# Pooled attention and a maxout FFN on one core: another fold of the first keys, chosen slots for the attention steps, one batch of loads at a time and five store buffers

## The chip, the cores and the metric

The kernel runs on 1 core of one Trainium2 chip. The metric is the device time of one execution in microseconds; less is better. The chip has eight cores, and seven stay idle here. A core has five engines that run beside one another, each with its own queue of instructions in a fixed order: TensorE (PE, matmuls; PEld are its weight loads), VectorE (DVE), ScalarE (ACT), GpSimd (POOL) and SyncE (SP), which here only issues transfers. Engines wait for one another by semaphores.

## The reference

```python
def _attn_ref(q, k, v):              # each 8 x 8 x 576 x 64: batch, heads, tokens, width
    pool = 8
    k_p = k.reshape(B, H, Sp, pool, D).mean(axis=3)      # Sp = 72
    v_p = v.reshape(B, H, Sp, pool, D).mean(axis=3)
    scores = scale * np.matmul(q, k_p.transpose(0, 1, 3, 2))
    scores = scores - np.max(scores, axis=-1, keepdims=True)
    attn = np.exp(scores)
    attn = attn / (np.sum(attn, axis=-1, keepdims=True) + 1e-09)
    return np.matmul(attn, v_p)

def _moe_ref(x, w1, w2, w3, w_out):  # x is 4608 x 512, w1..w3 512 x 768, w_out 768 x 512
    h = np.maximum(np.maximum(x @ w1, x @ w2), x @ w3)
    return h @ w_out
```

`x` is the output of the attention, its heads side by side: 8 batches of 576 tokens make 4608 rows. Keys and values are averaged over groups of 8 tokens, so a head has 72 of each. Inputs and output are float32.

## The kernel before

**Tiles.** The FFN runs over nine tiles of 512 tokens (`n` = 0 to 8), the attention over eight batches of 576 tokens. The loop for tile `n` also does the attention of batch `n + 1`, so that TensorE has dense work in between. Tiles 7 and 8 have no attention beside them.

**Attention of a batch.** `fold_k` and `fold_v` add the eight tokens of a group in three halvings; batch 0's keys on VectorE in three thirds (line 327), batches 2 to 7 on GpSimd, while `pool_k` and `pool_v` sum k and v of batch 1 and v of batch 0 by eight accumulating matmuls with an identity. `kp` holds the pooled keys twice; `turn_k` transposes them on TensorE into `pkt` and copies that into `kz` on two sets of rows, one after the other. `turn_q` transposes blocks of 128 queries into `pqt` and copies them to `qT`. `scores` makes one head's scores in `psc` and ScalarE's exponential writes them to `et`. `values` multiplies `et` with the pooled values (a column of eights gives the sum), and VectorE takes the reciprocal `rcp` and writes the scaled `xn`. `turn_x` transposes `xn` into `pxt` and ScalarE copies it to `xT`, the FFN's input.

**FFN of a tile.** `hidden` has a slot for each of 6 blocks of 128 hidden units and each of the three weight matrices: four accumulating matmuls into `pw`, then a copy on ScalarE (first matrix) or a maximum on VectorE (second and third, the third into `hT`). That is 18 slots; for tiles 0 and 1 the first two blocks run in two halves of 256 tokens, so that there are 24. `project` has four slots: six matmuls into `po`, a copy on ScalarE into the store buffer `osb` and two stores of 128 KB from SP (line 311).

**Banks and buffers.** PSUM has eight banks: three for `pw`, `po` and the start's transposes, two buffers of two banks ("att") for `psc` and `pav`, and one ("tr") that `pqt`, `pkt`, `pxt` and the poolings of batch 1 share. `osb` lies in a pool with three buffers (`sb3`, line 306); `kt`, `vt` and `qb` have two each.

**The order** is written by hand: the program order is the order in each engine's queue. Attention steps are generators that yield after each step; `queries(b)` followed by `outputs(b)` are 22 steps for a batch. Lines 401 to 424 take one step after each of the 22 slots of a tile (`todo`), in tile 1 only after six slots (`lead`), and after every slot a step of what is left over from batch 1 (`side`). At the start, `heat` runs matmuls on constant data into a bank that nobody reads.

**Loads.** q, k, v and weights are loaded from GpSimd's queue, which also folds; k 0, k 2 and v 2 come from SP. Ahead of the loop the loads of batches 3 and 4 are issued, and in the loop those of batch `n + 4` (lines 402 to 411), each behind the fold that frees its buffer.

Of the kernel before, what the change touches and what calls it, by code (L numbers as in the profile page):

```python
# [10 lines left out]
ALU = mybir.AluOpType  # L11
# [3 lines left out]
def kernel(  # L15
# [30 lines left out]
    JCH = DFF // 128  # L46
# [27 lines left out]
    def load_v(b, eng, dtype=F32, parts=1):  # L74
        vts[b] = ld.tile([Sp, H, POOL, D], dtype, name="vt", tag="vt")
        src = v[b].rearrange("h (sp j) d -> sp h j d", j=POOL)
        n = H // parts
        return [eng.dma_start(out=vts[b][:, h:h + n], in_=src[:, h:h + n])
                for h in range(0, H, n)][-1]
# [22 lines left out]
    nc.vector.memset(warm, 1.0)  # L102
    ident = const.tile([128, 128], BF16, name="ident", tag="ident")
    make_identity(nc, ident)
    load_v(0, nc.gpsimd, F16, 2)
    identh = const.tile([128, 128], F16, name="identh", tag="identh")
    make_identity(nc, identh)
    for i in range(3):
        load_w(slice(256 * i, 256 * i + 256))
    load_k(1, nc.gpsimd, F16)  # L110
# [31 lines left out]
    def fold_v(b):  # L142
        fold(nc.gpsimd, vts[b], [vp_all[:, b, :, 0:D]])

    def pool_v(b, h, tag, evac):

        pvp = psp.tile([128, 4, D], F32, name="pvp", tag=tag[0], bufs=tag[1])
        for j in range(POOL):
            nc.tensor.matmul(pvp, identh[0:Sp, :], vts[b][:, h:h + 4, j, :],  # L149
                             start=(j == 0), stop=(j == POOL - 1))  # L150
        evac(out=vp_all[:, b, h:h + 4, 0:D], in_=pvp[0:Sp])

    def turn_q(b, n0, n1, evac, tag):
        if b not in qTs:
            qTs[b] = sb2.tile([128, 2 * NG, 128], BF16, name="qT", tag="qT")
        pqt = psp.tile([128, n1 - n0, 128], BF16, name="pqt", tag=tag[0],
                       bufs=tag[1])
        qf = qbs[b].rearrange("p hp t d -> p (hp t d)")
        for n in range(n0, n1):
            nc.tensor.transpose(pqt[:, n - n0, :], qf[:, 128 * n:128 * n + 128],  # L160
                                ident)
        evac(out=qTs[b][:, n0:n1, :], in_=pqt)  # L162

    def turn_k(b, evacs, tag):
        pkt = psp.tile([128, 6, 96], BF16, name="pkt", tag=tag[0], bufs=tag[1])
        for i in range(6):
            nc.tensor.transpose(pkt[:, i, :], kps[b][:, i, :, :], ident[0:96, 0:96])  # L167
        for par in range(2):
            rows = slice(64 * par, 64 * par + 64)
            evacs[par](  # L170
                out=kz_all[b % 2][rows, par, :, 0:Sp].rearrange(
                    "p h (r i) -> p h r i", i=6),
                in_=pkt[rows].rearrange("p i (h r) -> p h r i", h=H))
# [58 lines left out]
    TR = ("tr", 1)  # L232
# [3 lines left out]
    def queries(b):  # L236

        new_et(b)
        if b == 1:
            pool_k(b, TR)  # L240
            yield
            turn_k(b, V_V, TR)
            yield
        for m in range(3):
            turn_q(b, 6 * m, 6 * m + 6, nc.scalar.copy, TR)
            yield
        if b > 1:
            turn_k(b, V_V, TR)
            yield
        for h in range(H):  # L250
            scores(b, h)
            yield
# [45 lines left out]
    def project(n, hT):  # L298
        for mm in range(4):
            m = 4 * n + mm  # L300
            po = psp.tile([128, C], F32, name="po", tag="pw", bufs=3)
            for jc in range(JCH):
                nc.tensor.matmul(po, hT[:, jc, bass.ts(mm, 128)],  # L303
                                 wo_sb[:, jc, :],
                                 start=(jc == 0), stop=(jc == JCH - 1))
            osb = sb3.tile([128, C], F32, name="osb", tag="osb")
            nc.scalar.copy(out=osb, in_=po)  # L307
# [12 lines left out]
    def heat(n):  # L320
        for _ in range(n):
            nc.tensor.matmul(wm, warm[:, 0:128], warm, start=True, stop=True)

    new_et(0)
    heat(14)
    for i in (0, 2, 4):
        fold_k(0, nc.vector, i, i + 2)
    turn_q(0, 0, 5, nc.scalar.copy, PW)
    turn_q(0, 5, 9, nc.scalar.copy, PW)
    heat(1)  # L330
    turn_k(0, (nc.vector.tensor_copy, nc.scalar.copy), PW)

    def scores4(h):
        psc = psp.tile([128, 4, 256], F32, name="psc4", tag="att", bufs=2)
        for i in range(4):
            score(0, h + i, psc[:, i, :], 0, 0, 4)
        exp(ets[0][:, h:h + 4, 0:256], psc[0:Sp])

    def scores2(h):
# [12 lines left out]
    pool_v(0, 0, PW, nc.vector.tensor_copy)  # L352
    scores2(2)
    pool_v(0, 4, PW, nc.vector.tensor_copy)
    scores2(4)
    heat(1)
    scores2(6)
    out0 = outputs(0, (PW, PW, TR, TR, TR))
    next(out0)
# [8 lines left out]

    nc.vector.memset(kz_all[1], 0.0)
    hT0 = new_hT()  # L370
    side = queries(1)
    steps = {16: 1, 17: 1, 19: 1, 20: 1, 21: 1, 22: 2, 23: 2}
# [5 lines left out]
    pool_v(1, 0, TR, nc.scalar.copy)  # L378
    next(side)
    next(side)  # L380
    pool_v(1, 4, TR, nc.scalar.copy)
    for _ in side:
        pass
    side = outputs(1)
# [16 lines left out]
    NSTEP = 3 + 1 + H + 5 + 5  # L401
    for n in range(1, TOK // NB):
        if n + 2 < B:
            fold_k(n + 2, nc.gpsimd)
            if n + 4 < B:
                load_k(n + 4, nc.gpsimd)
            fold_v(n + 2)
            if n + 4 < B:
                load_v(n + 4, nc.gpsimd)
        if n + 3 < B:  # L410
            load_q(n + 3)
        hT = new_hT()
        nxt = batch(n + 1) if n + 1 < B else iter(())
        lead = 6 if n == 1 else 0
        nslot = 3 * JCH + 4
        slot = -lead
        for part in (hidden(n, hT), project(n, hT)):
            for _ in part:
                next(side, None)
                if slot >= 0:  # L420
                    todo = (slot + 1) * NSTEP // nslot - slot * NSTEP // nslot
                    for _ in range(todo):
                        next(nxt, None)
                slot += 1
        for _ in nxt:
            pass
# [30 lines left out]
```

## Time and profile before

| what | us |
|---|---|
| median of 3 runs | 284.22 |
| the three runs | 282.95, 284.22, 291.58 |
| the profiled execution | 282.14 |
| its span | 280.3 |

| engine | busy us | share of the span | instructions |
|---|---|---|---|
| PE | 254.8 | 91% | 1837 |
| PEld | 139.3 | 50% | 1838 |
| DVE | 129.9 | 46% | 232 |
| ACT | 132.2 | 47% | 224 |
| POOL | 117.7 | 42% | 83 |

The span is what the hardware profiler saw between the first and the last instruction; the time of an execution has 1.8 us around it. The trace has starts and lengths of instructions, and for an engine that sat idle, what released it. The page cuts the span into 40 slices of 7 us: TensorE's and the DMA engines' busy share in tenths, and the clock that TensorE was granted. The DMA engines are busy in the first half and TensorE has holes in three places, the first two slices, slices 13 and 14, and the last one:

```profile
PE   7689999788992699999999999999999999999993
PEclk9799999999999599999999999999999999999998
DMA  7999998898999989979006500600060006006006
```

### The profile page before, as it was taken

The numbers are of one execution on the slowest core, as the hardware profiler recorded it, in microseconds if no ns is written. First come the engines' busy times: TensorE is split into PE (matmuls) and PEld (weight loads), VectorE is DVE, ScalarE is ACT, GpSimd is POOL, SyncE is SP. The second block draws the span as 40 slices with busy tenths as digits, with TensorE's granted clock in tenths as the row PEclk, the third lists the DMA queues.
The fourth block names the chain that finished last, engine by engine and source line by source line (L and its number), as shares of the span: only waits on it lengthen the run. The fifth ranks groups of instructions, "written<-read, shape, count | busy, mean of one in ns | idle before, by whom it ended". The sixth has DMA issues, their size and how long they took to land.

```text
span 280.3 us, 4602 instructions
## 1 busy us (share of the span) xinstructions
PE 254.8 (91%) x1837; PEld 139.3 (50%) x1838; DVE 129.9 (46%) x232; ACT 132.2 (47%) x224; POOL 117.7 (42%) x83
## 2 busy tenths in 40 slices
PE   7689999788992699999999999999999999999993
PEld 2468457564551345554555455545554554444441
DVE  5547553434640055625562556255625562531530
ACT  1464257555540456465646554655456544124122
POOL 8551004999699999938940993000000000000000
PEclk9799999999999599999999999999999999999998
DMA  7999998898999989979006500600060006006006
GB/s 184 201 196 206 201 237 190 217 235 146 207 227 238 263 183 188 225 183 210 14 4 150 84 4 2 150 0 0 10 143 2 0 13 139 0 1 152 0 1 150
DMA packets 20850, 34.71 MB, mean 124 GB/s; under 512 B 2620, under 2 KB 13244, under 8 KB 20252
## 3 DMA queue, kind: packets, MB, share of 16 engines
q0 software_dynamic: 14032, 21.44, 40.5%
q1 hardware_dynamic: 6796, 12.98, 19.2%
q8 instruction: 14, 0.23, 0.3%
q14 instruction: 8, 0.07, 0.1%
HBM read 34.60 MB, written 9.44 MB: 157 GB/s over the span
## 4 chain that ended last, share of the span: by engine, by line
PE 79%; DMA 9%; ACT 5%; DVE 4%; issue 2%; SPq 0%; ACTq 0%; POOLq 0%
PE pw L273 46%; PE po L303 14%; DMA out_dram<-osb 6%; PE psc L189 6%; DVE kz L170 3%; PE pqt L160 3%; PE pav L218 3%; PE pxt L209 3%; DMA qb<-in_q_dram 3%; ACT qT L162 2%; PE pvp L149 1%; PE pkt L167 1%; ACT t L278 1%; ACT xT L213 1%; ACT osb L307 1%
## 5 line engine op out<-in xcount | busy, mean ns | idle before, releaser
L273 PE MATMUL pw<-xT,mw 128*128 128x512 f16 (+1 forms) x696 | 161.5, 366 | 0.9 <-ACT xT L213 0.7
L273 PEld LDWEIGHTS <-mw 128*128 128x128 f16 x696 | 61.4, 98 | 47.7 <-issue 2.2
L281 DVE TENSOR_TENSOR t<-t,pw 128x512 f16<-128x512 f16 (+1 forms) x58 | 37.8, 651 | 80.6 <-PE pw L273 43.6
L303 PE MATMUL po<-mwo,hT 128*128 128x512 f16 x216 | 51.7, 379 | 0.1
L194 ACT ACTIVATE et<-psc 72x576 f16<-72x576 f32 (+2 forms) x62 | 40.4, 662 | 23.2 <-PE psc L189 23.0
L278 ACT CAST t<-pw 128x512 f16<-128x512 f32 (+1 forms) x58 | 32.3, 557 | 36.1 <-PE pw L273 33.0
L284 DVE TENSOR_TENSOR hT<-t,pw 128x512 f16<-128x512 f16 (+1 forms) x58 | 37.7, 650 | 18.5 <-PE pw L273 16.9
L128 POOL TENSOR_TENSOR vt<-vt 72x2048 f32<-72x2048 f32 (+1 forms) x12 | 41.2, 3433 | 2.8 <-DMA vt<-in_v_dram 2.3
L307 ACT COPY osb<-po 128x512 f32<-128x512 f32 x36 | 21.1, 586 | 44.2 <-PE po L303 31.7
L128 POOL TENSOR_TENSOR kt<-kt 96x1536 f32<-96x1536 f32 (+1 forms) x12 | 31.5, 2621 | 23.5 <-DMA kt<-in_k_dram 22.9
L213 ACT COPY xT<-pxt 128x512 f16<-128x512 f16 (+1 forms) x40 | 21.8, 546 | 19.4 <-PE pxt L209 19.4
L189 PE MATMUL psc<-qT,kz 128*128 128x64 bf16 (+3 forms) x192 | 27.1, 248 | 3.8 <-DVE kz L170 3.6
L303 PEld LDWEIGHTS <-hT 128*128 128x128 f16 x216 | 19.4, 97 | 19.3 <-DVE hT L284 0.7
L226 DVE TENSOR_TENSOR xn<-pav,rcp 128x512 f16<-128x512 f32 x40 | 27.7, 692 | 1.4
L189 PEld LDWEIGHTS <-kz 128*128 128x128 bf16 x192 | 17.6, 98 | 21.2 <-DVE kz L170 7.8
L162 ACT COPY qT<-pqt 128x768 bf16<-128x768 bf16 (+2 forms) x23 | 18.0, 786 | 17.4 <-PE pqt L160 17.4
L160 PE MATMUL pqt<-ident,qb 128*128 128x128 bf16 x144 | 13.3, 235 | 11.9 <-ACT xT L213 8.2
L160 PEld LDWEIGHTS <-qb 128*128 128x128 bf16 x144 | 10.9, 105 | 19.7 <-issue 14.8
L218 PEld LDWEIGHTS <-et 72*128 72x128 f16 x320 | 15.4, 98 | 8.3 <-issue 0.7
L224 DVE RECIPROCAL rcp<-pav 128x8 f32<-128x8 f32 x40 | 8.1, 204 | 24.3 <-PE pav L218 24.3
L209 PEld LDWEIGHTS <-xn 128*128 128x128 f16 x160 | 12.1, 98 | 10.6 <-issue 1.9
L218 PE MATMUL pav<-vp,et 72*128 72x65 f16 x320 | 16.8, 194 | 0.3 <-ACT et L194 0.3
(38 smaller groups left out, 111.4 us busy)
## 6 DMA issues: line engine op xcount, KB each, us to landing
out_dram<-osb SPq DMA_DIRECT2D x72, 128.0 KB, 2.4
kt<-in_k_dram POOLq DMA_DIRECT2D x5, 1152.0 KB, 11.9
vt<-in_v_dram POOLq DMA_DIRECT2D x5, 1152.0 KB, 12.7
qb<-in_q_dram POOLq DMA_DIRECT2D x7, 576.0 KB, 13.0
mw<-in_moe_w_dram POOLq DMA_DIRECT2D x9, 256.0 KB, 10.5
kt<-in_k_dram SPq DMA_DIRECT2D x3, 384.0 KB, 5.2
kt<-in_k_dram SPq DMA_DIRECT2D x1, 1152.0 KB, 10.4
vt<-in_v_dram SPq DMA_DIRECT2D x1, 1152.0 KB
```

What stands on the lines that cost most here:

```text
L128: e.tensor_tensor(out=t[:, :, 0:n, :], in0=t[:, :, 0:n, :], in1=t[:, :, n:2 * n, :], op=ALU.add)
L160: nc.tensor.transpose(pqt[:, n - n0, :], qf[:, 128 * n:128 * n + 128], ident)
L189: nc.tensor.matmul(out, kz_all[b % 2][:, f % 2, h, :], qTs[b][:, n + i0:n + i1, 64 * (h % 2):64 * (h % 2) + 64], start=True, stop=True)
L194: nc.scalar.activation(out=out, in_=in_, func=FT.Exp, scale=1.0 / 64.0)
L213: nc.scalar.copy(out=xT[:, :, g0 + keep:g0 + 128], in_=pxt[:, :, keep:128])
L218: nc.tensor.matmul(pav[:, h // 4, 65 * (h % 4):65 * (h % 4) + 65], ets[b][:, h, c0:c0 + 128], vp_all[:, b, h, :], start=True, stop=True)
L226: nc.vector.tensor_tensor(out=xn, in0=pv[:, :, :, 0:D], in1=rcp.to_broadcast([128, 2, 4, D]), op=ALU.mult)
L273: nc.tensor.matmul(pw, w_sb[wi][:, kc, bass.ts(jc, 128)], xT[:, kc, col], start=(kc == 0), stop=(kc == KCH - 1))
L278: nc.scalar.copy(out=t, in_=pw)
L281: nc.vector.tensor_tensor(out=t1, in0=t, in1=pw, op=ALU.max)
L284: nc.vector.tensor_tensor(out=hT[:, jc, c0:c1], in0=t, in1=pw, op=ALU.max)
L303: nc.tensor.matmul(po, hT[:, jc, bass.ts(mm, 128)], wo_sb[:, jc, :], start=(jc == 0), stop=(jc == JCH - 1))
```

## The change

It has four parts.

1. **Store buffers.** The tile `osb` is given five buffers instead of three.
2. **Loads.** The loads of batch 4 ahead of the loop are gone. In the loop, `fold_k(n + 2)` is followed by the load of k for batch `n + 3`, `fold_v(n + 2)` by those of v and q for batch `n + 3`.
3. **Slots.** A batch's queries are turned in four groups (5, 5, 4, 4 blocks) instead of three of 6, with the keys between the third and the fourth, so a batch has 23 steps. The lists `PLAN` and `PLAN1` (tile 1) name the slot of each step; the two steps that are left of batch 1 come after slots 0 and 2 of tile 1. For batch 1, in tile 0, the keys still come first, in slots 16 and 17, the four query groups in 19 to 22, two scores in 23 and six behind the last slot (before: three groups, two scores in slot 22, two in 23, four behind).
4. **Start.** k of batch 0 is folded once on VectorE (three adds of 4 tokens onto 4, into `k16`, float16), and the four sums are added by four matmuls with an identity per third. `spread` copies them to the two places of `kp` on VectorE and ScalarE. The keys are turned before the queries, the second half of q after the first four scores; v of batch 0 comes in three transfers and is pooled in three pieces. `heat` matmuls stand in between.

```diff
+    def load_v(b, eng, dtype=F32, cuts=(0, H)):
...
-    load_v(0, nc.gpsimd, F16, 2)
     identh = const.tile([128, 128], F16, name="identh", tag="identh")
     make_identity(nc, identh)
+    load_v(0, nc.gpsimd, F16, (0, 4, 6, 8))
...
     def queries(b):
         new_et(b)
-        if b == 1:
-            pool_k(b, TR)
-            yield
-            turn_k(b, V_V, TR)
-            yield
-        for m in range(3):
-            turn_q(b, 6 * m, 6 * m + 6, nc.scalar.copy, TR)
+        for m, (n0, n1) in enumerate(((0, 5), (5, 10), (10, 14), (14, 18))):
+            turn_q(b, n0, n1, nc.scalar.copy, TR)
             yield
-        if b > 1:
-            turn_k(b, V_V, TR)
-            yield
+            if m == 2 and b > 1:
+                turn_k(b, V_V, TR)
+                yield
...
-            osb = sb3.tile([128, C], F32, name="osb", tag="osb")
+            osb = sb3.tile([128, C], F32, name="osb", tag="osb", bufs=5)
...
+    def spread(i0, i1):
+        nc.vector.tensor_copy(out=kps[0][:, i0:i1, 0, :], in_=pkp0[0:96, i0:i1])
+        nc.scalar.copy(out=kps[0][:, i0:i1, 1, :], in_=pkp0[0:96, i0:i1])
+
     for i in (0, 2, 4):
-        fold_k(0, nc.vector, i, i + 2)
+        c = slice(i, i + 2)
+        nc.vector.tensor_tensor(out=k16[:, c], in0=kts[0][:, c, 0:4],
+                                in1=kts[0][:, c, 4:8], op=ALU.add)
+        for j in range(4):
+            nc.tensor.matmul(pkp0[:, c], identh[0:96, :], k16[:, c, j, :],
+                             start=(j == 0), stop=(j == 3))
+        if i == 2:
+            spread(0, 4)
+        else:
+            heat(1)
+    spread(4, 6)
+    heat(2)
+    turn_k(0, (nc.vector.tensor_copy, nc.scalar.copy), PW)
     turn_q(0, 0, 5, nc.scalar.copy, PW)
-    turn_q(0, 5, 9, nc.scalar.copy, PW)
-    heat(1)
-    turn_k(0, (nc.vector.tensor_copy, nc.scalar.copy), PW)
+    turn_q(0, 5, 9, nc.vector.tensor_copy, PW)
...
+    scores4(0)
     turn_q(0, 9, 14, nc.vector.tensor_copy, PW)
-    scores4(0)
     turn_q(0, 14, 18, nc.vector.tensor_copy, PW)
...
-    load_k(4, nc.gpsimd)
-    load_v(4, nc.gpsimd)
...
+    PLAN = (1, 2, 4, 5, 7, 8, 9, 10, 11, 12, 13, 14, 15, 16, 17, 17, 18, 18, 19, 19,
+            20, 20, 21)
+    PLAN1 = (7, 8, 10, 13, 14, 15, 16, 17, 18, 19, 20, 21, 22, 23, 24, 24, 25, 25, 26,
+             26, 27, 27, 27)
     for n in range(1, TOK // NB):
         if n + 2 < B:
             fold_k(n + 2, nc.gpsimd)
-            if n + 4 < B:
-                load_k(n + 4, nc.gpsimd)
+            if n + 3 < B:
+                load_k(n + 3, nc.gpsimd)
             fold_v(n + 2)
-            if n + 4 < B:
-                load_v(n + 4, nc.gpsimd)
-        if n + 3 < B:
-            load_q(n + 3)
+            if n + 3 < B:
+                load_v(n + 3, nc.gpsimd)
+                load_q(n + 3)
```

The rows below are instructions in the order of one engine's queue: source line, operation, output and inputs, shape; x2 stands for two alike in a row. The lines of the changed kernel differ from those of before by a few.

ScalarE at the start, from its first copy to the first three exponentials, before:

```order
L162 COPY qT<-pqt 128x640
L162 COPY qT<-pqt 128x512
L170 COPY kz_120<-pkt 64x8x72
L194 ACTIVATE et<-psc_186 72x4x256
L194 ACTIVATE et<-psc_199 72x4x256
L194 ACTIVATE et<-psc_205 72x2x320
```

and in the changed kernel:

```order
L326 CAST kp<-pkp 96x4x64
L326 CAST kp<-pkp 96x2x64
L169 COPY kz_121<-pkt 64x8x72
L161 COPY qT<-pqt 128x640
L193 ACTIVATE et<-psc_192 72x4x256
L193 ACTIVATE et<-psc_212 72x4x256
```

Two casts of `kp` came in front, the query copy moved behind the `kz` copy, and the second query copy went to VectorE.

ScalarE at the end of tile 0, from the last FFN copies to the first store buffers, before:

```order
L162 COPY qT<-pqt 128x768 x2
L278 CAST t_536<-pw_531 128x512
L162 COPY qT<-pqt 128x768
L194 ACTIVATE et<-psc 72x576 x4
L151 CAST vp<-pvp 72x4x64
L194 ACTIVATE et<-psc 72x576 x2
L151 CAST vp<-pvp 72x4x64
L194 ACTIVATE et<-psc 72x576 x2
L307 COPY osb<-po 128x512 x2
```

and in the changed kernel:

```order
L161 COPY qT<-pqt 128x640 x2
L272 CAST t_556<-pw_551 128x512
L161 COPY qT<-pqt 128x512 x2
L193 ACTIVATE et<-psc 72x576 x3
L150 CAST vp<-pvp 72x4x64
L193 ACTIVATE et<-psc 72x576 x2
L150 CAST vp<-pvp 72x4x64
L193 ACTIVATE et<-psc 72x576 x3
L301 COPY osb<-po 128x512 x2
```

There are four query copies instead of three, and one exponential less ahead of the first `vp` cast and one more behind the second.

VectorE at the end of tile 2, from the maximum of a late FFN slot through the values of batch 3, before:

```order
L284 TENSOR_TENSOR hT<-t_1317,pw_1324 128x512
L224 RECIPROCAL rcp<-pav 128x8
L226 TENSOR_TENSOR xn<-pav,rcp 128x512
L281 TENSOR_TENSOR t_1360<-t_1340,pw_1355 128x512
L224 RECIPROCAL rcp<-pav 128x8
L226 TENSOR_TENSOR xn<-pav,rcp 128x512
L284 TENSOR_TENSOR hT<-t_1360,pw_1375 128x512
```

and in the changed kernel:

```order
L275 TENSOR_TENSOR t_1391<-t_1379,pw_1386 128x512
L223 RECIPROCAL rcp<-pav 128x8
L225 TENSOR_TENSOR xn<-pav,rcp 128x512
L278 TENSOR_TENSOR hT<-t_1391,pw_1406 128x512
L223 RECIPROCAL rcp<-pav 128x8
L225 TENSOR_TENSOR xn<-pav,rcp 128x512
L223 RECIPROCAL rcp<-pav 128x8
```

The first `rcp` and `xn` of a batch stand behind the maximum of slot 16 instead of the one of slot 11, and the pairs of `rcp` and `xn` follow one another without FFN maxima in between.

More of the change, by code (lines that the diff above doesn't have):

```diff
@@ L72, in load_k @@
                 for i in range(0, 6, n)][-1]
-    def load_v(b, eng, dtype=F32, parts=1):
+    def load_v(b, eng, dtype=F32, cuts=(0, H)):
         vts[b] = ld.tile([Sp, H, POOL, D], dtype, name="vt", tag="vt")
         src = v[b].rearrange("h (sp j) d -> sp h j d", j=POOL)
-        n = H // parts
-        return [eng.dma_start(out=vts[b][:, h:h + n], in_=src[:, h:h + n])
-                for h in range(0, H, n)][-1]
+        return [eng.dma_start(out=vts[b][:, h:g], in_=src[:, h:g])
+                for h, g in zip(cuts, cuts[1:])][-1]
     def load_q(b):
@@ L143, in fold_v, with pool_v @@
         fold(nc.gpsimd, vts[b], [vp_all[:, b, :, 0:D]])
-    def pool_v(b, h, tag, evac):
-        pvp = psp.tile([128, 4, D], F32, name="pvp", tag=tag[0], bufs=tag[1])
+    def pool_v(b, h, g, tag, evac):
+        pvp = psp.tile([128, g - h, D], F32, name="pvp", tag=tag[0], bufs=tag[1])
         for j in range(POOL):
-            nc.tensor.matmul(pvp, identh[0:Sp, :], vts[b][:, h:h + 4, j, :],
+            nc.tensor.matmul(pvp, identh[0:Sp, :], vts[b][:, h:g, j, :],
                              start=(j == 0), stop=(j == POOL - 1))
-        evac(out=vp_all[:, b, h:h + 4, 0:D], in_=pvp[0:Sp])
+        evac(out=vp_all[:, b, h:g, 0:D], in_=pvp[0:Sp])
     def turn_q(b, n0, n1, evac, tag):
@@ L325 @@
     heat(14)
-    for i in (0, 2, 4):
-        fold_k(0, nc.vector, i, i + 2)
+    new_kp(0)
+    k16 = const.tile([96, 6, 4, D], F16, name="k16", tag="k16")
+    pkp0 = psp.tile([128, 6, D], F32, name="pkp", tag="pw", bufs=3)
+    def spread(i0, i1):
+        nc.vector.tensor_copy(out=kps[0][:, i0:i1, 0, :], in_=pkp0[0:96, i0:i1])
+        nc.scalar.copy(out=kps[0][:, i0:i1, 1, :], in_=pkp0[0:96, i0:i1])
+    for i in (0, 2, 4):
+        c = slice(i, i + 2)
[11 more added lines that the diff above has]
+    turn_k(0, (nc.vector.tensor_copy, nc.scalar.copy), PW)
     turn_q(0, 0, 5, nc.scalar.copy, PW)
-    turn_q(0, 5, 9, nc.scalar.copy, PW)
-    heat(1)
-    turn_k(0, (nc.vector.tensor_copy, nc.scalar.copy), PW)
+    turn_q(0, 5, 9, nc.vector.tensor_copy, PW)
     def scores4(h):
@@ L351 @@
     scores2(0)
-    pool_v(0, 0, PW, nc.vector.tensor_copy)
+    pool_v(0, 0, 4, PW, nc.vector.tensor_copy)
     scores2(2)
-    pool_v(0, 4, PW, nc.vector.tensor_copy)
+    pool_v(0, 4, 6, PW, nc.vector.tensor_copy)
     scores2(4)
-    heat(1)
+    pool_v(0, 6, 8, PW, nc.vector.tensor_copy)
     scores2(6)
@@ L370, with early @@
     hT0 = new_hT()
-    side = queries(1)
-    steps = {16: 1, 17: 1, 19: 1, 20: 1, 21: 1, 22: 2, 23: 2}
+    def early():
+        pool_k(1, TR)
+        yield
+        turn_k(1, V_V, TR)
+        yield
+        yield from queries(1)
+    side = early()
+    steps = {16: 1, 17: 1, 19: 1, 20: 1, 21: 1, 22: 1, 23: 2}
     for slot, _ in enumerate(hidden(0, hT0)):
@@ L377 @@
             next(side)
-    pool_v(1, 0, TR, nc.scalar.copy)
+    next(side)
+    pool_v(1, 0, 4, TR, nc.scalar.copy)
     next(side)
     next(side)
-    pool_v(1, 4, TR, nc.scalar.copy)
+    pool_v(1, 4, 8, TR, nc.scalar.copy)
     for _ in side:
@@ L399, in batch @@
         yield from outputs(b)
-    NSTEP = 3 + 1 + H + 5 + 5
+    PLAN = (1, 2, 4, 5, 7, 8, 9, 10, 11, 12, 13, 14, 15, 16, 17, 17, 18, 18, 19, 19,
+            20, 20, 21)
+    PLAN1 = (7, 8, 10, 13, 14, 15, 16, 17, 18, 19, 20, 21, 22, 23, 24, 24, 25, 25, 26,
+             26, 27, 27, 27)
     for n in range(1, TOK // NB):
@@ L404 @@
             fold_k(n + 2, nc.gpsimd)
-            if n + 4 < B:
-                load_k(n + 4, nc.gpsimd)
+            if n + 3 < B:
+                load_k(n + 3, nc.gpsimd)
             fold_v(n + 2)
-            if n + 4 < B:
-                load_v(n + 4, nc.gpsimd)
-        if n + 3 < B:
-            load_q(n + 3)
+            if n + 3 < B:
+                load_v(n + 3, nc.gpsimd)
+                load_q(n + 3)
         hT = new_hT()
         nxt = batch(n + 1) if n + 1 < B else iter(())
-        lead = 6 if n == 1 else 0
-        nslot = 3 * JCH + 4
-        slot = -lead
+        plan = PLAN1 if n == 1 else PLAN
+        slot = 0
         for part in (hidden(n, hT), project(n, hT)):
             for _ in part:
[L419 to L423, printed above, removed]
+                if slot in (0, 2):
+                    next(side, None)
+                for _ in range(plan.count(slot)):
+                    next(nxt, None)
                 slot += 1
```

## The prediction, made before the change was run

> **What bounds the kernel now.** I read the page's busy times first (TensorE busy 91% of the span), then the chain of waits, then cut the span at the first FFN matmul of each token tile and asked for the busy time in every stretch. The columns are the stretch, its length, then PE, PEld, DVE, ACT and POOL busy (instructions), the granted clock, the DMA share and GB/s.
>
> ```profile
> 0.00:20.87 20.87, 15.69 (x118) 9.21 (x120) 11.08 (x26) 8.86 (x12) 13.52 (x25) 0.92 1.16 194
> 20.87:52.83 31.96, 31.39 (x272) 20.06 (x272) 16.89 (x33) 16.07 (x30) 8.12 (x6) 1.00 1.11 211
> 52.83:84.69 31.86, 28.05 (x242) 17.43 (x240) 15.51 (x30) 16.91 (x30) 28.48 (x18) 1.00 0.95 204
> 84.69:122.21 37.52, 28.84 (x208) 15.51 (x206) 13.98 (x24) 15.55 (x26) 35.46 (x21) 0.91 0.95 215
> ...
> 150.10:178.01 27.91, 27.27 (x208) 14.63 (x205) 13.98 (x24) 15.55 (x26) 16.05 (x8) 1.00 0.31 60
> ...
> 233.83:280.30 46.47, 41.77 (x195) 18.59 (x192) 16.51 (x24) 12.58 (x22) 0.00 (x0) 0.98 0.25 57
> ```
>
> Tiles 2 to 6 do the same work, yet tile 2 takes 37.52 us and the next ones 27.9. The chain and the timeline say why (start, duration, what; in brackets the idle time and its releaser):
>
> ```profile
> 81.19 11.68 DMA out_dram<-osb
> ...
> 92.97 0.59 ACT L307 COPY osb<-po 128x512 f32<-128x512 f32 x1 [8.75 <-DMA out_dram<-osb]
> 93.45 0.38 ACT L213 COPY xT<-pxt 128x256 f16<-128x256 f16 x1
> ...
> 93.88 0.80 PE L160 MATMUL pqt<-ident,qb 128*128 128x128 bf16 x6 [8.17 <-ACT xT L213]
> 94.47 1.91 PE L273 MATMUL pw<-xT,mw 128*128 128x512 f16 x4
> ```
>
> The fourth copy of `osb` needs the first of three store buffers, whose store takes 11.68 us. ScalarE waits 8.75 us with the last `xT` copy queued behind, which holds the one `tr` bank, and so TensorE waits 8.17 us. After it the four matmuls of one slot take 1.91 us instead of about 1.03: the clock has dropped (0.91 over the stretch). The store is slow beside the loads (DMA share 0.95 in this stretch, 0.31 in tile 4); over the run the median to landing is 2.4 us, between 60 and 94 us it is 12.0:
>
> ```profile
> out_dram<-osb SPq DMA_DIRECT2D x72, 128.0 KB, 2.4
> ...
> out_dram<-osb SPq DMA_DIRECT2D x7, 128.0 KB, 12.0
> ```
>
> **A steady tile.** These rows price every step on TensorE: a slot of four FFN matmuls 0.86 us, six projecting ones 1.30, and by the differences of starts a head's scores 0.25, values 0.26, an output transpose 0.23, six query transposes 0.33.
>
> ```profile
> 163.16 0.86 PE pw L273 x4
> 172.06 1.30 PE po L303 x6
> ...
> 152.50 0.49 PE L160 MATMUL pqt<-ident,qb 128*128 128x128 bf16 x6
> 152.83 1.03 PE L273 MATMUL pw<-xT,mw 128*128 128x512 f16 x4
> ...
> 157.32 0.28 PE L189 MATMUL psc<-qT,kz 128*128 128x192 bf16 x2 [0.48 <-DVE kz L170]
> ...
> 158.30 0.41 PE L189 MATMUL psc<-qT,kz 128*128 128x320 bf16 x3
> 158.55 1.03 PE L273 MATMUL pw<-xT,mw 128*128 128x512 f16 x4
> ...
> 167.21 0.43 PE L218 MATMUL pav<-vp,et 72*128 72x65 f16 x8
> 167.47 1.03 PE L273 MATMUL pw<-xT,mw 128*128 128x512 f16 x4
> 168.33 0.39 PE L209 MATMUL pxt<-identh,xn 128*128 128x128 f16 x4
> 168.56 1.03 PE L273 MATMUL pw<-xT,mw 128*128 128x512 f16 x4
> ```
>
> Work of a tile: 18 x 0.86 + 4 x 1.30 + 8 x 0.25 + 5 x 0.26 + 5 x 0.23 + 3 x 0.33 + 0.25 (key transposes, taken as a head's scores) = 26.4 us. The tile takes 27.9, so 1.5 us are short waits, nearly all at its head, where query groups follow slot by slot through the single `tr` bank and the scores wait for `kz` (0.48).
>
> **The sum, part by part.** It is made against the profiled execution, 282.14 us, 2.1 below the median of 284.22.
>
> *Five store buffers, one batch of loads: -10.1 in tile 2.* A projection makes four stores; with five buffers its fourth copy needs a buffer last used in the tile before, some 25 us earlier, against 11.68 us for the slow store. The copy then waits for TensorE alone. Tile 2 falls from 37.52 to the new steady time of 27.4 (below). The loads that go out later cost nothing as long as each tile's data is folded in time (first rival). Ends: -8.2 (the pause alone) to -10.6.
>
> *Steps in chosen slots, tiles 3 to 6: -0.5 each, -2.0.* Query groups get a slot or two between them, so the copy that empties `tr` (1.18 us for nine blocks in the next fence, 0.65 for five) is covered by 0.86 or 1.7 us of FFN. What waits next: the key transposes stand in slot 5 and the fourth query group in slot 7, in the same bank. VectorE first does the maximum of slot 5, then two `kz` copies of 0.75 (row in the next fence): 0.2 + 0.69 + 1.5 = 2.4 us against 0.25 + 2 x 0.86 = 2.0 on TensorE, a wait of 0.5 with the semaphores. And at slot 17 an output transpose comes one slot after its values: 0.2 + 0.69 (maximum) + 0.2 (reciprocal, estimated from the gap between values and `xn`) + 0.69 (`xn`) = 1.85 us against 0.26 + 0.86 + 0.26 = 1.4: 0.5. New tile 26.4 + 1.0 = 27.4. In the projection slots ScalarE has two copies, 0.59 and about as much, for 1.8 us of TensorE, which covers them. Ends per tile: -1.3 (no wait) to +1.0 (each of the two waits doubled). Tile 2 has its share in the line above.
>
> *First k: +1.0 at the start.* Rows of the start:
>
> ```profile
> 6.45 1.13 DVE L128 TENSOR_TENSOR kt<-kt 96x512 f32<-96x512 f32 x2
> 8.84 1.14 PE L160 MATMUL pqt<-ident,qb 128*128 128x128 bf16 x9 [2.24 <-DMA qb<-in_q_dram]
> 9.60 1.18 ACT L162 COPY qT<-pqt 128x640 bf16<-128x640 bf16 x2 [7.58 <-PE pqt L160]
> 10.93 0.75 DVE L170 COPY kz<-pkt 64x576 bf16<-64x576 bf16 x1 [1.24 <-PE pkt L167]
> 11.61 0.47 DVE L162 COPY qT<-pqt 128x640 bf16<-128x640 bf16 x1
> 11.71 0.63 ACT L170 COPY kz<-pkt 64x576 bf16<-64x576 bf16 x1 [0.94 <-DVE kz L170]
> 12.83 3.40 ACT L194 ACTIVATE et<-psc 72x1024 f16<-72x1024 f32 x4 [0.48 <-PE psc L189]
> ...
> 20.87 0.60 PE L273 MATMUL pw<-xT,mw 128*128 128x256 f16 x4 [0.67 <-ACT xT L213]
> ```
>
> and of the shapes that the new work has or comes near to:
>
> ```profile
> L194 ACT ACTIVATE et<-psc 72x576 f16<-72x576 f32 x56 | 35.8, 647 | 22.1 <-PE psc L189 22.1
> L128 DVE TENSOR_TENSOR kt<-kt 96x512 f32<-96x512 f32 x3 | 2.0, 683 | 2.1 <-DMA kt<-in_k_dram 2.1
> L226 DVE TENSOR_TENSOR xn<-pav,rcp 128x512 f16<-128x512 f32 x40 | 27.7, 692 | 1.4
> L151 DVE CAST vp<-pvp 72x256 f16<-72x256 f32 x2 | 0.8, 422 | 2.5 <-PE pvp L149 2.5
> ```
>
> The twelve adds become three of 0.68. The second third of k was there at 6.45 at the latest: add to 7.1, four identity matmuls (0.33, as six transposes) to 7.5, cast on VectorE (0.42) to 8.1, and only then, by VectorE's order, the third add to 8.8, four matmuls to 9.1, a small cast on VectorE and after it one on ScalarE (0.3 each) to 9.9, key transposes, `kz` from 10.35 instead of 10.93. That is 0.6 gained, but the query copies now stand behind `kz`: ScalarE's `kz` runs 11.1 to 11.75, its query copy (0.69) to 12.45, the scores (0.45) follow, and the first exponential starts at 13.05 instead of 12.83. The second half of q is transposed only after these scores: copies on VectorE to 13.9 and 14.35, second exponential at 15.0 instead of about 13.9. Four more follow, with the split v pooling beside them as before, so the first FFN matmul moves from 20.87 to about 21.9. Ends: -0.6 (the lead of `kz` kept) to +1.9 (TensorE at half speed here).
>
> On that speed: nine transposes took 1.14 us after a pause of 2.24, where six take 0.49 later, so a pause of that length halved it. The new start fills the pause with sums and three `heat` matmuls; its pauses are under 1 us, and I take full speed, since a pause of 1.34 us in tile 1 (row below) lies in a stretch with clock 1.00. [...]
>
> *End of tile 0: +1.3.* The first two scores of batch 1 move from slot 22 to slot 23, so six scores instead of four lie outside the FFN. Between them are two poolings:
>
> ```profile
> 42.97 0.88 PE pvp L149 x8
> ```
>
> TensorE has 8 x 0.25 + 2 x 0.88 + 1.3 = 5.1 us from the first score to the first values. With two score buffers the eighth score must wait for the sixth exponential: 0.4 until the first one starts, six of 0.647 and two casts of 0.4, some 5.1 us after the first score began, plus its own 0.25 and the projection's 1.3: 6.6. The difference is 1.5, of which some 0.2 is there already (TensorE idles 0.57 us in the whole stretch). Ends: 0 to +1.6.
>
> *Tile 1: -1.7.*
>
> ```profile
> 53.65 0.59 ACT L307 COPY osb<-po 128x512 f32<-128x512 f32 x1 [1.81 <-DMA out_dram<-osb]
> ...
> 54.77 0.38 PE L209 MATMUL pxt<-identh,xn 128*128 128x128 f16 x4 [1.34 <-ACT xT L213]
> ```
>
> Its work is 26.4 + 0.45 (two output transposes of batch 1) = 26.9 against 31.86. The store wait goes. New waits, by the same reckoning: 0.5 for the first output transpose, 0.45 between query groups in slots 7 and 8 (only a half slot of 0.43 between), 1.4 for the fourth query group one slot behind the keys, 0.95 for the last output transpose right behind its values: 3.3. So 30.2. Ends: -3 to 0.
>
> The tail (tiles 7 and 8) is not touched. Sum: 282.14 - 10.1 - 2.0 + 1.0 + 1.3 - 1.7 = 270.6; rounded up to 271, since the runs of before lie above the profiled one.
>
> **Rivals.** *Loads too late (slower).* One batch ahead, GpSimd's loop is: k lands, k is folded (an estimated half of POOL's 16.05 us in a tile, 8), the next k is issued.
>
> ```profile
> DMA to landing us min/median/max: 4.1/9.5/19.4
> ```
>
> With the longest landing of before (19.4) the loop takes 27.4 us, just a tile; with the median 17.5. Above that each further microsecond costs one per tile over five tiles, so 2% slower needs landings of 24 us: 271 + 5 x 4.6 = 294. Against it: fewer loads share the DMA engines than in the run that gave 19.4. 3%.
>
> *Short waits eat the gain.* If the other three values and output transposes in the projection wait 0.5 as the first does, five tiles lose 7.5: 278.5. For it: two steps now share a slot. Against it: a 1.30 us projection covers 0.2 + 0.69 on VectorE, which has no other work there. 15%, two thirds of it below 278.5.
>
> *The stall stays,* because the copy was held by something other than the buffer, the store queue for instance: 271 + 9.7 = 280.7. The row names the store of the same buffer, landing 0.1 us before. 4%.
>
> *Start and tile 0 lose nothing:* 271 - 2.3 = 268.5. 8%.
>
> **The numbers.** The forecast holds 70%, with 269 to 274 as its own range. The range 267.5 to 276 leaves out the upper half of the waits, the stall and the late loads, under 2 in 10. A measurement of this kernel tells 2% from no change, 278.5 to 289.9 here. Faster: 70 + 8 + 10 = 88%; the same: 5 + 4 = 9%; slower 3%.
>
> **What would show it.** Right: no `osb` wait on a store anywhere, tile 2 as long as tile 3, tiles of about 27.4 us with one wait before the fourth query group (released by `kz`) and one before the first output transpose (released by `xn`), the first FFN matmul near 21.9, a pause of TensorE behind exponentials at the end of tile 0. Wrong: TensorE waiting for `qb`, `kp` or `vp` in tiles 2 to 6, slow stores still in the chain, tiles above 28.5 us, or a first FFN matmul before 20.5.

## The result, and the profile after

The changed kernel takes 269.13 us (median of 4 runs, 268.88 to 269.91). The ratio to the kernel before, run beside it, is 0.9495, with a 95% interval of 0.9445 to 0.9544. Some runs of the kernel before, here and below, lie at 289 to 293 us, most of them at a lower granted clock (0.958 to 0.964, where the others have 0.967 to 0.985); the ratios leave such runs out. The profiled execution took 269.02 us, with a span of 267.3.

The forecast was 271.0 us (267.5 to 276.0), faster. By parts, from the start of a tile's first FFN matmul to that of the next, in the two profiled executions:

| part | before | after | difference | predicted |
|---|---|---|---|---|
| start | 20.87 | 20.83 | 0.0 | +1.0 |
| tile 0 | 31.96 | 33.21 | +1.25 | +1.3 |
| tile 1 | 31.86 | 30.17 | -1.69 | -1.7 |
| tile 2 | 37.52 | 27.36 | -10.16 | -10.1 |
| tiles 3 to 6, together | 111.62 | 109.43 | -2.2 | -2.0 |
| tiles 7 and 8 | 46.47 | 46.30 | -0.2 | 0 |

The differences add up to -13.0, and 282.14 - 13.0 is 269.1.

The page's slices of the changed kernel (each 6.7 us). TensorE's hole in slices 13 and 14 is gone, and the clock stays in its top digit until the last slice:

```profile
PE   7598998998998999999999999999999999999993
PEclk9999999999999999999999999999999999999998
DMA  7999999698757958969777604200330033006006
```

The stretches of the changed kernel, cut as before at each tile's first FFN matmul: length, then PE, PEld, DVE, ACT and POOL busy (instructions), clock, DMA share, GB/s.

```profile
0.00:20.83 20.83, 15.14 (x138) 9.56 (x141) 9.63 (x21) 9.08 (x13) 14.28 (x26) 1.00 1.16 195
20.83:54.04 33.21, 31.63 (x273) 20.14 (x273) 16.90 (x33) 16.54 (x32) 9.59 (x9) 1.00 1.08 208
54.04:84.21 30.17, 27.62 (x241) 17.44 (x238) 15.60 (x30) 17.10 (x32) 28.74 (x15) 1.00 0.73 174
84.21:111.57 27.36, 26.88 (x208) 14.77 (x205) 13.90 (x24) 15.15 (x27) 25.71 (x16) 1.00 0.92 211
111.57:138.92 27.35, 26.87 (x207) 14.74 (x205) 13.90 (x24) 15.61 (x28) 23.32 (x14) 1.00 0.78 184
```

Tile 2 (the fourth row) is as long as tile 3, although its DMA share is 0.92, about what it was before (0.95). TensorE's busy time fell only from 28.84 to 26.88; the other 8.2 us of the gain were idle.

TensorE's waits and their releasers in the changed kernel (total us, times, longest):

```profile
PE pqt L159 <- DVE kz L169: 2.3, 6, 1.2
PE pxt L208 <- DVE xn L225: 2.1, 6, 0.8
...
PE psc L188 <- ACT et L193: 1.0, 2, 0.5
```

These are three of the waits that the prediction reckoned for the tiles: the fourth query group behind `kz`, an output transpose behind `xn`, and at the end of tile 0 the scores behind the exponentials. No transfer is among TensorE's releasers. ScalarE's waits with `osb` all end on the projection's matmul, none on a store:

```profile
ACT osb L301 <- PE po L297: 30.5, 36, 2.4
```

### The profile page after: what moved, and what is told of

It reads as the page before. It is cut to its first block, busy times and chain, and to the rows that moved or that the text cites. A ratio compares the mean times of both kernels' runs of the same rounds, so it can differ in the third digit from the quotient of the medians.

```text
span 267.3 us, 4638 instructions
## 1 busy us (share of the span) xinstructions
PE 250.4 (94%) x1858; PEld 139.6 (52%) x1860; DVE 128.1 (48%) x227; ACT 132.9 (50%) x232; POOL 117.7 (44%) x84
## 4 chain that ended last, share of the span: by engine, by line
PE 83%; DVE 9%; ACT 5%; issue 1%; DVEq 0%; ACTq 0%
PE pw L267 45%; PE po L297 17%; PE psc L188 6%; PE pxt L208 4%; PE pqt L159 3%; DVE kz L169 3%; PE pav L217 3%; PE wm L316 3%; ACT et L193 2%; DVE xn L225 2%; DVE t L275 2%; ACT t L272 1%; PE pvp L148 1%; DVE hT L278 1%; ACT qT L161 1%
## 5 line engine op out<-in xcount | busy, mean ns | idle before, releaser
L267 PE MATMUL pw<-xT,mw 128*128 128x512 f16 (+1 forms) x696 | 157.2, 364 | 0.9 <-ACT xT L212 0.7
L267 PEld LDWEIGHTS <-mw 128*128 128x128 f16 x696 | 62.2, 98 | 50.9 <-issue 1.2
L188 PE MATMUL psc<-qT,kz 128*128 128x64 bf16 (+3 forms) x192 | 25.4, 246 | 3.1 <-ACT qT L161 1.7
L161 ACT COPY qT<-pqt 128x640 bf16<-128x640 bf16 (+1 forms) x29 | 18.6, 641 | 18.1 <-PE pqt L159 18.1
L208 PE MATMUL pxt<-identh,xn 128*128 128x128 f16 x160 | 15.5, 219 | 2.3 <-DVE xn L225 2.1
L159 PEld LDWEIGHTS <-qb 128*128 128x128 bf16 x144 | 9.9, 97 | 11.4 <-DVE kz L169 5.3
```

The costliest lines, as they stand in the source:

```text
L188: nc.tensor.matmul(out, kz_all[b % 2][:, f % 2, h, :], qTs[b][:, n + i0:n + i1, 64 * (h % 2):64 * (h % 2) + 64], start=True, stop=True)
L208: nc.tensor.transpose(pxt[:, kc, :], xn[:, kc // 2, 2 * (kc % 2):2 * (kc % 2) + 2, :], identh)
L267: nc.tensor.matmul(pw, w_sb[wi][:, kc, bass.ts(jc, 128)], xT[:, kc, col], start=(kc == 0), stop=(kc == KCH - 1))
```

## Experiments

Kernel by kernel: first the parts alone, then the changed kernel with one part undone, then what is left to gain. The ratios are to the kernel before, from runs on the same chip, with 95% intervals.

**1. Five buffers alone.** The kernel before with this line alone changed:

```diff
-            osb = sb3.tile([128, C], F32, name="osb", tag="osb")
+            osb = sb3.tile([128, C], F32, name="osb", tag="osb", bufs=5)
```

> The kernel before with five store buffers and nothing else. Theory A (the ring of store buffers makes the stall): no copy into a store buffer waits for a store, tile 2 falls from 37.5 to 27.9 us and the wait at the end of tile 0 (1.3 us) goes, so about 282.1 - 9.6 - 1.3 = 271.2 us, although the stores themselves stay slow (about 12 us between 60 and 94 us). Rival B (the loads in flight are the cause, and one batch at a time is what helps): most of the stall stays, 278 us or more.

270.48 us (270.30 to 271.15), ratio 0.9529 (0.9478 to 0.9580): nearly all of the gain. In the profiled executions 9.6 us of it lie in tile 2 and 1.1 in tile 1; 0.9 more come from a start that kept its clock (1.00 between 9 and 11 us, where it was 0.50 before; 19.95 us, see the account of the start below) and do not belong to the buffers. Tile 2 is as long as the others, while the DMA engines are busier than in the changed kernel (its stretch of tile 2, DMA share 0.99, and then its stores issued between 60 and 94 us):

```profile
82.67:110.58 27.91, 27.22 (x208) 14.63 (x205) 13.99 (x24) 15.54 (x27) 26.50 (x16) 1.00 0.99 222
```

```profile
out_dram<-osb SPq DMA_DIRECT2D x8, 128.0 KB, 14.7
```

The stores are slower here than before (median 14.7 against 12.0 us), and nothing waits for them. What cost the 9.6 us was not the slow store but the copy that needed its buffer.

**2. Four buffers alone.** The same line with `bufs=4`.

> The kernel before with four store buffers instead of three, nothing else changed. If the stall comes from the fourth copy of a tile needing the buffer of the first copy of the same tile, four buffers move that to the tile before, about 25 us earlier, which is more than the longest landing seen (17 us): no wait of a store buffer on a store, 270.5 as with five. If depth in itself matters because stores queue up over more than one tile, a wait remains around tile 2 and the time lies at 273 to 280.

271.18 us (270.97 to 271.42), ratio 0.9597 (0.9577 to 0.9617). Again all 36 waits of `osb` end on the projection, and tiles 1 to 8 are as long as with five buffers to 0.02 us. The profiled execution is 0.7 longer because its start is (20.68 against 19.95 us, see the section on the hardware). One buffer more than before is enough, since the fourth copy of a tile then needs the buffer of a copy that was made a whole tile earlier.

**3. Loads alone.** The kernel before with the changed loads, still three buffers:

```diff
-    load_k(4, nc.gpsimd)
-    load_v(4, nc.gpsimd)
...
-            if n + 4 < B:
-                load_k(n + 4, nc.gpsimd)
+            if n + 3 < B:
+                load_k(n + 3, nc.gpsimd)
```

(v likewise; q, which was loaded for batch `n + 3` already, goes out behind v.)

> The kernel before with the loads one batch at a time, still three store buffers. Theory A: the stores of tile 1 still run beside some loads; in the changed kernel they took up to 8.7 us, so the fourth copy waits about 4 us in place of 8.75, and the time lies between 273 and 278 us. Rival B: the stores land in time, no copy waits, tile 2 takes 27.9 us: 271 to 272 us.

285.66 us (281.99 to 294.0, 10 runs), ratio 1.0042 (0.9996 to 1.0089): no gain, against both expectations. ScalarE's rows at the end of tiles 2 and 3, from two places of the timeline:

```profile
117.74 0.58 ACT L307 COPY osb<-po 128x512 f32<-128x512 f32 x1 [5.45 <-DMA out_dram<-osb]
...
150.78 0.58 ACT L307 COPY osb<-po 128x512 f32<-128x512 f32 x1 [4.41 <-DMA out_dram<-osb]
```

and its stretches of tiles 2, 3 and 4:

```profile
84.82:112.73 27.91, 27.27 (x208) 14.63 (x206) 13.99 (x24) 15.53 (x26) 25.60 (x16) 1.00 0.89 208
112.73:146.80 34.07, 28.70 (x208) 15.49 (x206) 13.99 (x24) 15.53 (x26) 24.37 (x14) 0.95 0.72 166
146.80:179.82 33.02, 28.71 (x208) 15.47 (x206) 13.98 (x24) 15.54 (x26) 16.06 (x8) 0.95 0.34 74
```

Tile 2 runs through, but the loads that now go out later meet the stores of the next two projections: in the page's slices that hold the slow ones the DMA engines are busy 0.9 and 0.7, then 0.7 and 0.4. The store that the first of these copies waited for stands in the chain of waits, and took 8.38 us, against 11.68 before (the second copy's took 7.34):

```profile
109.26 8.38 DMA out_dram<-osb
```

One stall of 9.6 us became two of 6.2 and 5.1 (34.07 and 33.02 against 27.9), and over each of the two stretches the clock is at 0.95, where tile 2 has 1.00.

**4. The changed kernel with three buffers.**

> The changed kernel with three store buffers instead of five. Theory A: the fourth copy of tile 1 waits again, 2 to 4 us, and TensorE with it: 271 to 273.5 us. Rival B: the loads part alone has removed the stall: 269 us as in the changed kernel.

272.85 us at the median, but the four runs spread: 270.01, 276.13, 270.75 and 274.96, so no difference can be named. In the profiled run, the shortest, the fourth copy of tile 2 (not of tile 1, as expected) comes late, and tile 3 takes 28.49 us instead of 27.36:

```profile
113.36 0.59 ACT L301 COPY osb<-po 128x512 f32<-128x512 f32 x1 [2.69 <-PE pw L267]
```

The view names a matmul of `pw`, but the copy reads `po`, whose matmuls were done at 111.34. What is left is the buffer of the tile's first copy, whose `po` matmuls were done at 106.00: its stores would have had 6.7 us to land, an estimate from these times and the 0.59 of a copy, and the longest landing in this run was 9.2. (The one wait of `osb` that the view does put down to a store, 1.0 us, is in tile 7.) With three buffers the time hangs on how the stores land; in each of the nine kernels here that have four or five, the four runs lie within 1.12 us. How the other parts soften the stall beside experiment 3 was not separated.

**5. The changed kernel with the old loads**, the diff of experiment 3 undone, five buffers.

> The changed kernel with the loads two batches ahead as before, five store buffers kept. Theory A: the stores are slow again (about 12 us) but nobody waits for them: 269 us, within 0.5. Rival B: the traffic costs time in some other place as well: 271 us or more.

269.48 us (268.86 to 269.86), ratio 0.9487 (0.9434 to 0.9540). Stores between 60 and 94 us take 14.0 us at the median instead of 8.2, tiles 0 to 7 are as long to 0.01 us, and no copy waits for a store. With enough buffers the part on the loads is worth nothing.

**6. The changed kernel with the old start**: twelve adds on VectorE in place of three and the sums, and the old order of queries, keys and v.

> The changed kernel with the start of before (first keys folded three times on VectorE, queries turned before keys, v of batch 0 in two transfers). By the prediction's term the old start is 1.0 us earlier: 268 us. By the traces (first FFN matmul at 20.83 after and 20.87 before) it is the same: 269 us, within 0.5, with the granted clock of the first stretch back at about 0.92.

269.07 us (268.31 to 269.23), ratio 0.9474 (0.9428 to 0.9521). The first FFN matmul comes at 20.70, against 20.83. By this pair the new start is worth nothing.

**7. The changed kernel with the old slots**: three query groups with the keys behind them, two scores of batch 1 in slot 22 again, and one step after each slot of a tile.

> The changed kernel with the order of steps of before (three query groups, one step after each slot, batch 1 with four scores behind tile 0's last slot). By the prediction's terms: tiles 2 to 6 at 27.9 us each instead of 27.3 (+2.7), tile 0 shorter by 1.3, tile 1 about the same: 270.4 us. Rival: the slots bring nothing (269) or bring the larger part of what the stall did not (272 or more).

271.72 us (271.23 to 271.97), ratio 0.9571 (0.9526 to 0.9616): 2.6 more than the changed kernel, 1% of the time. Tile 0 is 31.95, tile 1 30.76 and tiles 2 to 6 27.91 each, so the slots cost 1.26 in tile 0 and give 0.59 + 5 x 0.55 = 3.3 behind it, 2.1 in sum. The other 0.6 us are its start (21.47), where the 14 `heat` matmuls at the beginning ran to 7.4 us instead of 6.8 and the first sums queued behind them. Tiles 7 and 8 are as in the changed kernel, so their 0.2 us do not come from the slots. They lie in tile 7 (20.95 us before, 20.72 in the changed kernel); the cause stays open.

**8. The changed kernel without `heat` between the first sums.**

```diff
         if i == 2:
             spread(0, 4)
-        else:
-            heat(1)
     spread(4, 6)
-    heat(2)
```

> The changed kernel without the four warming matmuls that stand between the sums of the first keys (one after the first third, one after the last, two before the key transposes). Theory: with TensorE idle most of the time between 7 and 9.5 us the granted clock falls to one half around 9 us, as it did before after a pause of 2.24 us, and the first FFN matmul comes 0.5 to 1 us later: 269.5 to 270. Rival: the sums alone keep the clock, and the shorter queue brings it forward by up to 0.6: 268.4 to 269.

269.61 us (269.12 to 270.24), ratio 0.9500 (0.9450 to 0.9550). In the profiled execution the first FFN matmul comes at 21.70, 0.9 later; tiles 0 to 7 are as they were.

```profile
11.00:12.00 1.00, 0.09 (x1) 0.09 (x1) 0.00 (x0) 0.84 (x2) 0.40 (x1) 1.00 1.29 194
12.00:13.00 1.00, 1.00 (x12) 0.95 (x12) 0.03 (x1) 0.45 (x1) 0.76 (x2) 0.75 1.41 197
13.00:14.00 1.00, 1.00 (x7) 0.61 (x5) 0.82 (x2) 0.56 (x1) 1.00 (x2) 0.50 1.45 196
```

The clock falls in the thirteenth microsecond, where the changed kernel keeps 1.00. These matmuls are worth up to 0.9 us, though the medians differ by 0.5 only.

**9. Keys through another bank.** The wait of the fourth query group, taken away: the keys of batches 2 to 7 are transposed into a score buffer, not into `tr`.

```diff
+    ATT = ("att", 2)
...
-                turn_k(b, V_V, TR)
+                turn_k(b, V_V, ATT)
```

> The changed kernel with the key transposes of batches 2 to 7 written to one of the two score buffers instead of the single shared bank. Theory: the wait before the fourth query group (1.16 us in tile 1, about 0.4 in tiles 2 to 6) is for that bank alone, and goes: 269.0 - 1.2 - 2.0 = 265.9 us. Rival: the wait moves to the first scores, which need kz or the score buffer: 268.5 us or more.

265.89 us (265.81 to 266.07), ratio 0.9369 (0.9316 to 0.9421): as forecast. Tile 1 is 28.98 (-1.2) and tiles 2 to 6 26.95 each (-0.41), and the row `pqt` behind `kz` is gone from TensorE's waits.

**10. All three waits taken away.** Experiment 9, and: batch 1's keys through the score buffer too, its steps in tile 0 one slot closer so that two scores lie in slot 22 again, the last output transpose in a bank of `pw`, values at slots 16 and 17 and outputs from slot 18.

```diff
-    steps = {16: 1, 17: 1, 19: 1, 20: 1, 21: 1, 22: 1, 23: 2}
+    steps = {16: 1, 17: 1, 18: 1, 19: 1, 20: 1, 21: 1, 22: 2, 23: 2}
...
-    next(side)
...
-        yield from outputs(b)
+        yield from outputs(b, (TR, TR, TR, TR, PW))
...
-    PLAN = (1, 2, 4, 5, 7, 8, 9, 10, 11, 12, 13, 14, 15, 16, 17, 17, 18, 18, 19, 19,
-            20, 20, 21)
+    PLAN = (1, 2, 4, 5, 7, 8, 9, 10, 11, 12, 13, 14, 15, 16, 17, 18, 18, 19, 19, 20,
+            20, 21, 21)
```

(In `PLAN1` likewise; there the query groups also come in slots 4, 6, 8 and 11 instead of 7, 8, 10 and 14, and the keys in 10 instead of 13. The expectation speaks of the keys of tile 0 three slots earlier; in tile 0 the edit moves the query groups and scores by one slot, and in tile 1 the keys by three.)

> The changed kernel with the keys of every batch from 1 on turned through a score buffer, the last output transpose of a batch in a pw bank, the keys of tile 0 three slots earlier in the order so that two scores lie in slot 22 and two in 23 again, and the values at slots 16 and 17 with the outputs from slot 18 on. If the waits of the changed kernel come from the one shared bank and from a step that follows its producer by one slot, all of them go: tile 0 is 1.0 to 1.3 us shorter (about 32.0), tile 1 about 28.2, tiles 2 to 6 about 26.5, in all 261.5 to 263.5. If the projection's slots are already full, the outputs moved behind slot 18 give new waits there: tiles 2 to 6 stay at 26.95 or longer, in all 264 to 267.

261.30 us (261.21 to 261.74), ratio 0.9252 (0.9226 to 0.9278), the shortest of all, 7.8 us under the changed kernel. Its stretches:

```profile
20.79:52.66 31.87, 31.16 (x272) 20.14 (x272) 16.89 (x33) 16.41 (x32) 8.69 (x7) 1.00 1.09 214
52.66:80.35 27.69, 27.37 (x242) 17.42 (x239) 15.50 (x30) 16.36 (x31) 26.00 (x15) 1.00 0.80 187
80.35:106.87 26.52, 26.52 (x207) 14.72 (x205) 13.89 (x24) 15.47 (x28) 25.47 (x16) 1.00 0.82 177
```

In tile 2 TensorE's busy time equals the stretch. 26.5 us is the work of a tile that the prediction added up from rows (26.4). TensorE's waits of over 0.2 us that are left in this kernel lie at the start, but for the last row (batch 1's keys in tile 0):

```profile
PE psc L188 <- ACT qT L161: 1.7, 1, 1.7
PE pkp L334 <- DVE k L331: 1.5, 2, 1.1
PE wm L317 <- DVE warm L101: 1.5, 1, 1.5
PE pw L268 <- ACT xT L212: 0.7, 1, 0.7
PE pkt L166 <- ACT kp L182: 0.3, 1, 0.3
```

## Why the prediction was right, and where it was not

None of the three rivals that were to cost time came about: TensorE waits for no transfer (loads too late), the projection's later slots show no waits in tiles 2 to 6 (short waits), and no copy waits for a store (the stall). Step by step:

*Tile 2, -10.1 (measured -10.16).* Right, mechanism and size: the copy needed a buffer whose store was still under way (experiments 1 and 2); that is 9.6 us, and the chosen slots give the other 0.55. But the prediction booked the gain on buffers and loads together, and the loads have no share in it: alone they move the stall (3), and without them nothing is lost (5).

*Tiles 3 to 6, -0.5 each (measured -0.55).* Right, and both waits are where it put them. The changed kernel's rows in tile 2:

```profile
90.51 1.89 PE L267 MATMUL pw<-xT,mw 128*128 128x512 f16 x8
92.63 0.40 PE L159 MATMUL pqt<-ident,qb 128*128 128x128 bf16 x4 [0.23 <-DVE kz L169]
...
103.80 0.42 PE L217 MATMUL pav<-vp,et 72*128 72x65 f16 x8
104.47 0.40 PE L208 MATMUL pxt<-identh,xn 128*128 128x128 f16 x4 [0.25 <-DVE xn L225]
```

Two slots are 1.72 us from start to start, so the query group could have begun at 92.23, and the output transpose, 0.26 after the values, at 104.06: 0.40 and 0.41 where 0.5 each was reckoned. (The brackets say less, because they count from the modelled end of the matmuls ahead.) Taking them away gave as much: 0.41 in experiment 9, and 0.43 more in experiment 10.

*End of tile 0, +1.3 (measured +1.25).* Right. TensorE's two pauses there in the changed kernel:

```profile
42.85 0.41 PE L188 MATMUL psc<-qT,kz 128*128 128x320 bf16 x3 [0.49 <-ACT et L193]
...
46.63 0.41 PE L188 MATMUL psc<-qT,kz 128*128 128x320 bf16 x3 [0.51 <-ACT et L193]
```

By starts they are 0.65 and 0.67 us. The prediction had one wait in mind, for the last score; from the first of the eight scores to the first values it reckoned 6.6 us, and it took 6.47 (41.70 to 48.17). With two scores back in slot 22 the tile is 31.87 (experiment 10), which is 1.34 less and below the 31.96 of before.

*Tile 1, -1.7 (measured -1.69).* Right, in sum and in the waits. Experiment 1 alone takes 1.1 off tile 1 (30.75), the store wait; the slots take 0.6 more (experiment 7: 30.76 against 30.17). Two of its four new waits were put at 1.4 (the fourth query group) and 0.95 (the last output transpose):

```profile
63.46 1.03 PE L267 MATMUL pw<-xT,mw 128*128 128x512 f16 x4
65.65 0.40 PE L159 MATMUL pqt<-ident,qb 128*128 128x128 bf16 x4 [1.16 <-DVE kz L169]
...
82.79 0.39 PE L208 MATMUL pxt<-identh,xn 128*128 128x128 f16 x4
83.98 0.40 PE L208 MATMUL pxt<-identh,xn 128*128 128x128 f16 x4 [0.80 <-DVE xn L225]
```

By starts, with 0.86 for the slot and 0.22 for the transpose ahead, they are 1.33 and 0.97. The other two were put at 0.5 (an output transpose of batch 1) and 0.45 (between query groups):

```profile
54.88 0.38 PE L208 MATMUL pxt<-identh,xn 128*128 128x128 f16 x4 [0.24 <-ACT xT L212]
...
59.60 0.44 PE L159 MATMUL pqt<-ident,qb 128*128 128x128 bf16 x5 [0.34 <-ACT qT L161]
```

The matmuls ahead of them start at 54.04 and 58.66 and take 0.43 for a half slot, so these waits are 0.41 and 0.51. The four add up to 3.22 us, where 3.3 was reckoned.

*Start, +1.0 (measured 0.0).* The step that failed. The order is as predicted, the durations were too long. ScalarE in the changed kernel:

```profile
10.77 0.63 ACT L169 COPY kz<-pkt 64x576 bf16<-64x576 bf16 x1 [1.13 <-DVE kz L169]
...
12.81 1.02 ACT L193 ACTIVATE et<-psc 72x1024 f16<-72x1024 f32 x1 [0.68 <-PE psc L188]
14.38 3.70 ACT L193 ACTIVATE et<-psc 72x1024 f16<-72x1024 f32 x5 [0.55 <-PE psc L188]
```

`kz` on ScalarE came at 10.77 (put at 11.1), the first exponential at 12.81 (13.05), the second at 14.38 (15.0), and from there to the first FFN matmul it took 6.45 us (6.9). So 0.3 of the 1.07 us were won by the time of `kz`, where the second add began at 6.31 (put at 6.45), the third was done at 8.50 (8.8) and the last cast at 9.64 (9.9). Another 0.3 were won by the second exponential: the two query copies ahead of it were done on VectorE at 13.91, and were put at 14.35. The last 0.45 lie behind it, where the prediction took over the pace of before, in which ScalarE waits once more for scores:

```profile
16.68 1.29 ACT L194 ACTIVATE et<-psc 72x640 f16<-72x640 f32 x2 [0.45 <-PE psc L189]
```

In the changed kernel the last five exponentials have no such wait between them (the last row above).

That the new start then costs nothing is in part luck, since the profiled start of before, against which the term was reckoned, was itself slow. TensorE's clock in it between 9 and 11 us:

```profile
9.00:11.00 2.00, 2.00 (x19) 1.72 (x18) 0.72 (x4) 1.18 (x2) 1.17 (x2) 0.50 1.24 201
```

Where the same old start kept its clock (experiment 1) its first FFN matmul came at 19.95, and against that the new start does cost 0.9. Against an old start that lost its clock, as in the profile before and in experiment 6 (0.50 between 9 and 11 us in both), it costs nothing. The four runs of experiment 6 fit this: three with a granted clock of 0.989 to 0.991 took 269.04 to 269.23 us, one with 1.000 took 268.31. The prediction gave the new start full speed because its pauses would be under 1 us. The speed came true and the reason did not: TensorE pauses there for 1.11 and 1.72 us, and the clock stayed at 1.00. Its fourth rival ("start and tile 0 lose nothing") came true for the start alone.

The sum (270.6) was 1.6 above the profiled execution, 1.0 for the start and 0.2 each in tiles 3 to 6 and in the last two; the rounding up to 271 added 0.4. The median lies inside the range and 0.1 above the forecast's own lower end.

## What to carry to other kernels

When a copy waits for a store, ask first how many copies lie between two uses of the same buffer, and how long the slowest store takes beside loads (11.68 us before, where the median of the run was 2.4): here one more buffer gave 4% by itself, while moving the loads alone only moved the stall. The bank that several kinds of transposes share made the fourth query group wait for the keys' copies, even with two slots of FFN between them (0.40 us in tile 2); a second bank for one kind gave another 1.2% (265.89 against 269.13). For a steady tile, add up TensorE's work from rows and compare with the tile: the difference is what an order can still gain, and here nearly all of it could be had (26.52 us in experiment 10, for 26.4 of work).

## What the runs showed of the hardware

TensorE's clock at the start does not hang on the length of a pause alone. The same old start is in experiments 1 and 2; stretches of the first and then of the second:

```profile
9.00:11.00 2.00, 1.52 (x19) 0.87 (x16) 1.61 (x5) 1.38 (x3) 1.25 (x2) 1.00 1.25 201
```

```profile
10.00:11.00 1.00, 0.73 (x7) 0.61 (x7) 0.72 (x1) 0.70 (x2) 0.49 (x1) 0.62 1.24 205
11.00:12.00 1.00, 0.97 (x6) 0.43 (x5) 0.49 (x1) 0.39 (x1) 0.25 (x1) 0.50 1.28 195
```

and TensorE's rows ahead of them, again of each:

```profile
8.56 0.68 PE L160 MATMUL pqt<-ident,qb 128*128 128x128 bf16 x9 [1.88 <-DMA qb<-in_q_dram]
```

```profile
8.78 0.68 PE L160 MATMUL pqt<-ident,qb 128*128 128x128 bf16 x9 [1.49 <-DMA qb<-in_q_dram]
...
10.27 0.72 PE L160 MATMUL pqt<-ident,qb 128*128 128x128 bf16 x5 [0.34 <-DMA qb<-in_q_dram]
```

With a pause of 1.88 us the clock stayed at 1.00, with pauses of 1.49 and 0.34 it fell to 0.50, and the first FFN matmul came 0.7 later (20.68 against 19.95).

In experiment 8 TensorE was busy for 1.50 of the four microseconds from 7.00 on and for 0.09 of the next, all at 1.00, before the clock fell to 0.75 and 0.50; its longest pause there was 1.72 us:

```profile
9.53 0.67 PE L159 MATMUL pqt<-ident,qb 128*128 128x128 bf16 x9
11.91 0.60 PE L188 MATMUL psc<-qT,kz 128*128 128x256 bf16 x4 [1.72 <-ACT qT L161]
```

The changed kernel has a pause of the same 1.72 us at the same place, ahead of its first scores at 12.17. It was busy for 2.35 of those four microseconds and 0.00 of the next, and its clock stayed at 1.00. What makes the clock fall, the runs do not show.
